# The two products of the channel-mixing block by seven block products instead of eight, in chunks of 768 tokens

## The chip, the cores and the metric

One core of a Trainium2 chip. The core has a matrix engine (TensorE; PE in the rows, its weight loads PEld), VectorE (DVE), ScalarE (ACT), GpSimd (POOL) and SyncE (SP), which in this kernel issues every DMA. The metric is the device time of one execution in microseconds, median of the runs.

## The reference, cut to what matters

Pooled attention, a first mixing block, then a second one; the change is in the last two lines of the second:

```python
def _moe2_ref(x, w_tok1, w_tok2, w_ch1, w_ch2):      # x: 8 x 576 x 512
    xt = x.transpose(0, 2, 1)
    h = np.maximum(xt @ w_tok1, 0.0) @ w_tok2
    u = x + h.transpose(0, 2, 1)
    h2 = np.maximum(u @ w_ch1, 0.0) @ w_ch2          # 512 x 1536, 1536 x 512
    return (u + h2).astype(np.float32)
```

The weights of both blocks come as 64-bit floats and are turned into 32-bit ones on the chip. There are 8 x 576 = 4608 tokens.

## The kernel before

Each big product is made of three matmuls on split operands: a number is held as a high part in the reduced type fp32r and a remainder, and high x high, high x low and low x high are added up in PSUM (HL3, line 61). All matmuls go through the helper mm, so all of them have line 159, transposes line 165; groups are told apart by the names of their tiles.

Stages: attention and first token mixing, batch by batch (lines 747 to 780); then for each of the 8 batches the first block's channel product (emit_ch, line 856), transposes (emit_tr), and the second block's token products (emit_tok1, emit_tok2), called from the loop at lines 1200 to 1218, where the next batch's u is loaded (load_u) and split (split_u, lines 853 and 854); the result goes to the DRAM buffer scr_x (line 918). In this text this second stretch, from about 553 to 776.6 us, is the token stage and one pass of its loop a batch.

The last stage (lines 1225 to 1235) takes the 4608 tokens in 9 chunks of 512. load_c fetches a chunk, split_c (lines 975 and 976) splits it, emit_c1 makes each of 12 hidden blocks of 128 rows from 12 matmuls and evicts it with a relu on ScalarE and a remainder on VectorE (lines 1003 and 1004), and emit_c2 makes each of 4 output blocks from 36 matmuls, adds u (line 1018) and stores (line 1019). The hidden result stays in SBUF. The weights are read as 64-bit words and converted in pieces of 256 or 288 columns by cq_step (VectorE lines 240 to 259, remainder on GpSimd or VectorE at line 287), partly in the token stage, partly in the first chunk.

SBUF tiles are named by tags, one buffer each, in one pool; a tile that takes over a tag waits for the last use of the one before. The eight PSUM banks are taken in turn by bank_any. Engines run in order; the order on each engine is set by a scheduler when the program is built, which starts from the order of the source but moves an instruction ahead when what it needs is there.

## Time and profile before

| | us |
|---|---|
| median of 3 runs | 1383.62 |
| lowest, highest | 1381.26, 1386.32 |
| span of the profiled execution | 1378.8 |
| of it the last stage, first to last matmul | 598.1 |

The profiled execution is known by its span; its own device time was not listed apart from the three runs. In the rows below, "x432" is a number of instructions, a tile name is the program's without its buffer number (so "m", "t", "x" stand for PSUM banks), and after "|" stand busy time, mean ns of one, and idle time before with what ended it. Windows list, after the length, the busy us of PE, PEld, DVE, ACT and POOL with the number of instructions, then the granted TensorE clock as a share of 2.4 GHz, the mean busy share of the 16 DMA engines, and GB/s.

### The profile page before, as it was taken

Reading aid. Unit: us, or ns where it says so; the run is one execution under the profiler, and the core shown is the slowest. Engines: PE = TensorE matmul, PEld = TensorE weight load, DVE = VectorE, ACT = ScalarE, POOL = GpSimd, SP = SyncE. Lnnn points to the kernel's source line nnn. Section 1 sums busy time; section 2 is a strip of 40 time slices with the busy share of each in tenths; the row PEclk is TensorE's granted clock in tenths of the full one; section 3 lists DMA queues with packets and bytes.
Section 4 is the critical chain, followed back from the end, with each engine's and each line's share of the span. In section 5 each row is a group of like instructions: output and inputs, shape, how many; then the busy total and the mean of one; then the engine's idle time right before and its main releaser. Section 6 shows DMA issues by size and latency. Waiting matters only on the chain.

```text
span 1378.8 us, 19219 instructions
## 1 busy us (share of the span) xinstructions
PE 1337.9 (97%) x7744; PEld 1179.0 (86%) x7744; DVE 708.7 (51%) x1473; ACT 441.5 (32%) x848; POOL 227.2 (16%) x251
## 2 busy tenths in 40 slices
PE   5999999999999999999999999999999999999998
PEld 3579999999999989899999888888888888888887
DVE  7698667595776898897445931212112221212120
ACT  4675455555545553242212321111111110102020
POOL 4363423243252442110000100000000000000000
PEclk9699999999999999999999999999999999999999
DMA  8324222132311124443211601010101010101000
GB/s 320 138 63 133 65 90 97 58 104 72 100 65 49 52 87 149 152 153 134 104 69 44 203 11 54 16 46 16 46 16 47 23 40 23 39 23 39 23 8 31
DMA packets 52297, 103.39 MB, mean 75 GB/s; under 512 B 5296, under 2 KB 6320, under 8 KB 52208
## 3 DMA queue, kind: packets, MB, share of 16 engines
q1 hardware_dynamic: 52208, 102.16, 22.1%
q8 instruction: 61, 1.00, 0.3%
q14 instruction: 28, 0.23, 0.1%
HBM read 73.83 MB, written 28.31 MB: 74 GB/s over the span
## 4 chain that ended last, share of the span: by engine, by line
PE 75%; DVE 16%; ACT 3%; issue 2%; DMA 2%; POOL 1%; SPq 0%; DVEq 0%; POOLq 0%; ACTq 0%
PE x L159 31%; PE m L159 21%; PE t L159 20%; PE x L165 2%; DVE sm L556 2%; DVE e L545 1%; DVE mx L544 1%; DVE tmp L725 1%; DVE sm L557 1%; DVE R L778 1%; DVE pt L595 1%; DMA stg<-w_ch 1%; DVE bdk L395 1%; DVE sums L402 0%; DMA bdk<-w_ch 0%
## 5 line engine op out<-in xcount | busy, mean ns | idle before, releaser
L159 PE MATMUL m<-wtk,Z 128*128 128x256 f32 (+1 forms) x1536 | 249.1, 301 | 9.4 <-DVE R L778 9.2
L159 PEld LDWEIGHTS m<-wtk,Z 128*128 128x128 f32 x1536 | 219.3, 191 | 12.2 <-DVE R L778 9.8
L159 PE MATMUL x<-Xh,wc 128*128 128x512 f32 x432 | 108.5, 392 | 0.0
L1003 ACT ACTIVATE gz<-m 128x512 fp32r<-128x512 f32 x18 | 10.7, 597 | 291.2 <-PE m L159 290.9
L159 PEld LDWEIGHTS x<-Xh,wc 128*128 128x128 f32 x432 | 81.0, 188 | 19.0
L740 POOL TENSOR_TENSOR Z<-tmp,Z 128x1024 fp32r<-128x1024 f32 x31 | 74.7, 2410 | 105.5 <-ACT Z L739 105.5
L159 PE MATMUL x<-gz,wc 128*128 128x512 f32 x324 | 91.5, 390 | 0.0
L1018 DVE TENSOR_TENSOR c<-x,c 128x512 f32<-128x512 f32 x18 | 12.4, 691 | 136.8 <-PE x L159 136.8
L159 PE MATMUL t<-wth,Xh 128*128 128x256 f32 (+1 forms) x504 | 76.3, 293 | 0.5 <-DVE Xh L528 0.2
L159 PEld LDWEIGHTS x<-gz,wc 128*128 128x128 f32 x324 | 60.8, 188 | 14.1
L159 PEld LDWEIGHTS t<-wth,Xh 128*128 128x128 f32 x504 | 66.9, 188 | 4.5 <-DVE Xh L528 1.8
L159 PE MATMUL x<-bdk,q 128*128 128x144 f32 x320 | 47.9, 303 | 14.9 <-DVE bdk L1055 7.0
L1004 DVE SCALAR_TENSOR_TENSOR gz<-x,gz 128x512 fp32r<-128x512 f32 x36 | 24.9, 691 | 67.0 <-ACT gz L1003 66.9
L159 PEld LDWEIGHTS x<-bdk,q 128*128 128x128 f32 x320 | 44.5, 203 | 17.2 <-issue 14.0
L159 PE MATMUL x<-Xl,wc 128*128 128x512 f32 x216 | 59.1, 395 | 0.0
L159 PE MATMUL m<-wtk,zt 128*128 128x256 f32 (+1 forms) x192 | 57.3, 298 | 0.0
L725 DVE TENSOR_TENSOR tmp<-x,tmp 128x1024 f32<-128x1024 f32 x32 | 39.0, 1219 | 31.3 <-ACT tmp L701 16.2
L159 PE MATMUL t<-Xh,wc 128*128 128x512 f32 x216 | 54.3, 393 | 0.0
L159 PE MATMUL m<-Xh,wc 128*128 128x512 f32 x216 | 54.2, 393 | 0.0
L707 DVE SCALAR_TENSOR_TENSOR tmp<-tmp,t 128x512 f32<-128x512 f32 x40 | 27.3, 682 | 47.4 <-ACT tmp L694 47.4
L561 POOL TENSOR_TENSOR e<-e,sm 128x720 f32<-128x720 f32 x32 | 45.2, 1413 | 27.8 <-DVE sm L560 26.1
L159 PEld LDWEIGHTS t<-Xh,wc 128*128 128x128 f32 x216 | 40.5, 188 | 9.5
(357 smaller groups left out, 2933.4 us busy)
## 6 DMA issues: line engine op xcount, KB each, us to landing
stg<-w_ch SPq DMA_DIRECT2D x38, 256.0 KB, 2.9
scr_u<-R SPq DMA_DIRECT2D x32, 288.0 KB, 2.1
u<-scr_u SPq DMA_DIRECT2D x32, 288.0 KB, 3.7
scr_x<-u SPq DMA_DIRECT2D x32, 288.0 KB, 2.3
c<-scr_x SPq DMA_DIRECT2D x36, 256.0 KB, 3.7
out<-c SPq DMA_DIRECT2D x36, 256.0 KB, 2.0
q<-qT SPq DMA_DIRECT2D x14, 640.0 KB, 3.9
kr<-kT SPq DMA_DIRECT2D x12, 576.0 KB, 3.9
```

The source lines that it names most:

```text
L159: nc.tensor.matmul(out=o, lhsT=l, rhs=r, start=start, stop=stop)
L165: nc.tensor.transpose(o, i, ident)
L395: nc.vector.tensor_copy(out=bdk[pr, 2 * g:2 * g + 2, 72 * e:72 * e + 72], in_=ks[pr])
L544: nc.vector.tensor_reduce(out=mx[:, c0:c1, :], in_=v, axis=AX.X, op=ALU.max)
L545: nc.vector.tensor_tensor(out=e[:, c0:c1, 2 * p:2 * p + 2, :], in0=v, in1=mx[:, c0:c1, :].unsqueeze(3).to_broadcast([128, n, 2, 72]), op=A ...
L556: nc.vector.tensor_reduce(out=sm, in_=ep, axis=AX.X, op=ALU.add)
L557: nc.vector.tensor_scalar(out=sm, in0=sm, scalar1=1e-9, scalar2=8.0, op0=ALU.add, op1=ALU.mult)
L561: nc.gpsimd.tensor_tensor(out=ep, in0=ep, in1=sm.unsqueeze(3).to_broadcast([128, 5, 2, 72]), op=ALU.mult)
L707: nc.vector.scalar_tensor_tensor(out=t, in0=t, scalar=MAGIC, in1=pt, op0=ALU.subtract, op1=ALU.subtract)
L725: nc.vector.tensor_tensor(out=tmp, in0=px.unsqueeze(1).to_broadcast([128, 2, 512]), in1=tmp, op=ALU.mult)
L740: later(1.0 if lo is nc.vector else 0.0, lambda: lo.tensor_sub(out=zl, in0=zv, in1=zh.bitcast(F32)), tg, zg)
L1004: nc.vector.scalar_tensor_tensor(out=g[:, 1, 0:n], in0=o, scalar=0.0, in1=g[:, 0, 0:n].bitcast(F32), op0=ALU.max, op1=ALU.subtract,)
```

## The change

Both products of the last stage are cut into 2 x 2 blocks: tokens in two halves of 384, contraction and output rows in halves. Seven products of sums and differences of blocks replace the eight block products; their results are combined when PSUM is evicted. A11, A12, A22 are blocks of the weights, S1 to S4 sums of such blocks; for each of them stands a like combination of the moving operand, made by moving().

Weights: weight_steps reads the 64-bit words of four blocks, converts them, forms the four sums, splits all seven into high and low part and stores them to DRAM (scr_w). These 72 steps are called one at a time by wstep between the groups of the token stage. The old conversions of these weights are gone.

channel_mix runs in a new pool that is laid over the old one, with waits per tile. It holds 34 buffers of 128 x 768 for moving operands, 12 of 128 x 384 for evictions and 21 weight tiles. First all six chunks go through the first product (first_pair: six groups of hidden rows, seven block products of six matmuls each); the hidden result goes to DRAM (scr_g). Then all six go through the second product (second_chunk), whose operands are read back from scr_g, combined and split again. pump takes the next steps of operand preparation from a queue whenever buffers are free. The weights of the second product replace those of the first in its last chunk.

```diff
-    sb = ctx.enter_context(tc.tile_pool(name="sb", bufs=1))
+    sbx = ExitStack()
...
+    NH = 384
+    NCH = NTOK // (2 * NH)
+    A12, A22, S1, S2, S3, S4, A11 = range(7)
+    PO = (A11, S2, A12, S1, S3, S4, A22)
+    scr_w = [dr.tile([128, 3, 7, 2, 2, 256], F32, name=f"scr_w{i}") for i in range(2)]
+    scr_g = [dr.tile([128, 4, 6, NH], F32, name=f"scr_g{c}") for c in range(NCH)]
...
+        def conv(i, kk):
+            if kk == 0:
+                raw[i][1] = wt_tile([128, 2, 2, 256], F32, f"wm{i}")
+            t = raw[i][0][kk]
+            m = raw[i][1][:, kk]
+            mu = m.bitcast(U32)
+            nc.scalar.activation(out=m, in_=t[:, :, :, 1].bitcast(F32), func=ACTF.Abs)
+            nc.vector.tensor_scalar(out=m, in0=m, scalar1=F64_FLOOR, scalar2=None, op0=ALU.max)
+            nc.vector.tensor_scalar(
+                out=mu, in0=mu, scalar1=3, scalar2=0x3FFFFFFF,
+                op0=ALU.logical_shift_left, op1=ALU.bitwise_and,
+            )
+            nc.vector.scalar_tensor_tensor(
+                out=mu, in0=t[:, :, :, 1], scalar=0xC0000000, in1=mu,
+                op0=ALU.bitwise_and, op1=ALU.bitwise_or,
+            )
+            nc.vector.scalar_tensor_tensor(
+                out=mu, in0=t[:, :, :, 0], scalar=29, in1=mu,
+                op0=ALU.logical_shift_right, op1=ALU.bitwise_or,
+            )
+        def sums(i):
+            m = raw[i][1]
+            s = raw[i][2] = wt_tile([128, 4, 256], F32, f"wsum{i}")
+            a11, a21, a12, a22 = m[:, 0, 0], m[:, 0, 1], m[:, 1, 0], m[:, 1, 1]
+            nc.gpsimd.tensor_tensor(out=s[:, 0], in0=a21, in1=a22, op=ALU.add)
+            nc.gpsimd.tensor_tensor(out=s[:, 2], in0=a11, in1=a21, op=ALU.subtract)
+            nc.vector.tensor_sub(out=s[:, 1], in0=s[:, 0], in1=a11)
+            nc.vector.tensor_sub(out=s[:, 3], in0=a12, in1=s[:, 1])
+        def split(i, half):
+            m, s = raw[i][1:3]
+            parts = ((m[:, 1], 2, nc.gpsimd), (m[:, 0, 0:1], 1, nc.gpsimd)) if half == 0 else (
+                (s[:, 0:2], 2, nc.vector), (s[:, 2:4], 2, nc.vector))
+            if half == 0:
+                raw[i][3] = {}
+            _, g, j = quads[i]
+            dst = scr_w[quads[i][0]]
+            for n, (src, k, eng) in enumerate(parts):
+                o = wt_tile([128, 2, 2, 256], F32R, f"wo{i}_{half}{n}")[:, 0:k]
+                nc.scalar.copy(out=o[:, :, 0], in_=src)
+                eng.tensor_sub(out=o[:, :, 1], in0=src, in1=o[:, :, 0].bitcast(F32))
+                o0 = (A12, A11)[n] if half == 0 else (S1, S3)[n]
+                nc.sync.dma_start(out=dst[:, g, o0:o0 + k, j], in_=o.bitcast(F32))
+        steps = [lambda: load(0)]
+        for i in range(len(quads)):
+            if i + 1 < len(quads):
+                steps.append(lambda i=i: load(i + 1))
+            steps += [lambda i=i: conv(i, 0), lambda i=i: conv(i, 1), lambda i=i: sums(i),
+                      lambda i=i: split(i, 0), lambda i=i: split(i, 1)]
+        return steps
...
+    def channel_mix(sc):
+        layout = ["b%d" % i for i in range(3)] + ["ev%d" % i for i in range(12)] + [
+            "b%d" % i for i in range(20, 30)] + ["wa%d" % i for i in range(7)] + [
+            "b%d" % i for i in range(3, 14)] + ["b%d" % i for i in range(30, 34)] + [
+            "b%d" % i for i in range(14, 18)] + ["wa7", "wa8", "b18", "b19"] + [
+            "wa%d" % i for i in range(9, 21)]
+        shapes = {"b": [128, 2, NH], "e": [128, NH], "w": [128, 2, 2, 256]}
+        for tag in layout:
+            sc.tile(shapes[tag[0]], F32, tag=tag, name=tag)
+        free_b = ["b%d" % i for i in range(34)]
+        free_e = ["ev%d" % i for i in range(12)]
+        free_w = ["wa%d" % i for i in range(21)]
+        class Buf:
+            def __init__(self, pool, dt, name):
+                self.pool = pool
+                self.tag = pool.pop(0)
+                self.t = sc.tile(shapes[self.tag[0]], dt, tag=self.tag, name=name)
...
+        def load_w(m, o, g):
+            w = weights[m, o, g] = Buf(free_w, F32R, f"wa{m}_{o}_{g}")
+            nc.sync.dma_start(out=w.t.bitcast(F32), in_=scr_w[m][:, g, o])
...
+        def split(key, x):
+            h, l = buf("h", F32R), buf("l", F32R)
+            ops[key] = (h, l)
+            nc.scalar.copy(out=h.t, in_=x.t)
+            nc.vector.tensor_sub(out=l.t, in0=x.t, in1=h.t.bitcast(F32))
+        def sub(o, x, y):
+            nc.vector.tensor_sub(out=o.t, in0=x.t, in1=y.t)
...
+            groups = [
+                [sp(A11, "11", False)],
+                [(0, t1), (1, t2), sp(S2, "t2", False)],
+                [sp(A12, "21", False), (0, t4)],
+                [sp(S1, "11", True)],
+                [(0, t3), sp(S3, "12", True)],
+                [sp(S4, "22", True)],
+                [sp(A22, "21", True)],
+            ]
+            return [ld(b) for b in ("11", "12", "22", "21")], groups
+        queue = []
+        def pump(n):
+            while queue and n > 0 and queue[0][0] <= len(free_b):
+                queue.pop(0)[1]()
+                n -= 1
...
+        for c in range(NCH):
+            loads, groups = moving(load_x(c), (0, c))
+            queue += loads + [s for g in groups for s in g]
...
+        def product(o, xs, first, last, cont):
+            seq = [(wx[wi], x[a]) for a, wi in HL3 for wx, x in xs]
+            for i, (l, r) in enumerate(seq):
+                mm(o, l, r, first and i == 0, last and i == len(seq) - 1, cont)
+        pump(15)
+        for g in range(3):
+            for o in PO:
+                load_w(0, o, g)
+        order2 = [(o, g) for o in PO for g in range(3)]
+        pump(4)
...
+        def first_pair(c, i):
+            g = i // 2
+            cs = slice((i % 2) * 128, (i % 2) * 128 + 128)
+            fin = c == NCH - 1
+            def prod(o, ps, first):
+                w = weights[0, o, g].t
+                h, l = ops[0, c, o]
+                xs = [((w[:, k, 0, cs], w[:, k, 1, cs]), (h.t[:, k], l.t[:, k])) for k in range(2)]
+                product(ps, xs, first, True, not first)
+                if i == 5:
+                    h.free()
+                    l.free()
+                if fin and i % 2 == 1:
+                    weights[0, o, g].free()
+                    load_w(1, *order2.pop(0))
+                pump(1 if not fin else 2)
+            def put(k, e):
+                nc.sync.dma_start(out=scr_g[c][:, k, i], in_=e.t)
+                e.free()
+            X = bank_any()[:, 0:NH]
+            prod(A11, X, True)
+            p1 = evac("p1")
+            nc.scalar.copy(out=p1.t, in_=X)
+            Y = bank_any()[:, 0:NH]
+            prod(S2, Y, True)
+            u2 = evac("u2")
+            nc.vector.tensor_add(out=u2.t, in0=Y, in1=p1.t)
+            p1.free()
+            prod(A12, X, False)
+            e = evac("g11")
+            nc.scalar.activation(out=e.t, in_=X, func=ACTF.Relu)
+            put(0, e)
+            W = bank_any()[:, 0:NH]
+            prod(S1, W, True)
+            p5 = evac("p5")
+            nc.scalar.copy(out=p5.t, in_=W)
+            Z = bank_any()[:, 0:NH]
+            prod(S3, Z, True)
+            nc.vector.tensor_add(out=p5.t, in0=Z, in1=p5.t)
+            nc.gpsimd.tensor_tensor(out=p5.t, in0=p5.t, in1=u2.t, op=ALU.add)
+            nc.scalar.activation(out=p5.t, in_=p5.t, func=ACTF.Relu)
+            put(3, p5)
+            prod(S4, W, False)
+            e = evac("g12")
+            nc.vector.tensor_add(out=e.t, in0=W, in1=u2.t)
+            nc.scalar.activation(out=e.t, in_=e.t, func=ACTF.Relu)
+            put(1, e)
+            prod(A22, Z, False)
+            e = evac("g21")
+            nc.vector.tensor_add(out=e.t, in0=Z, in1=u2.t)
+            u2.free()
+            nc.scalar.activation(out=e.t, in_=e.t, func=ACTF.Relu)
+            put(2, e)
...
+        def load_o(c, d, k, t):
+            e = evac("o")
+            t0 = (2 * c + t) * NH
...
+        def second_chunk(c):
+            D = range(2)
+            def prod(o, ps, first):
+                for ph in range(3):
+                    w = weights[1, o, ph].t
+                    h, l = ops[1, c, ph, o]
+                    for d in D:
+                        cs = slice(d * 128, d * 128 + 128)
+                        xs = [((w[:, k, 0, cs], w[:, k, 1, cs]), (h.t[:, k], l.t[:, k])) for k in range(2)]
+                        product(ps[d], xs, first and ph == 0, ph == 2, not first)
+                    h.free()
+                    l.free()
+                    pump(3)
...
+            X = banks()
+            u11 = [load_o(c, d, 0, 0) for d in D]
+            prod(A11, X, True)
+            p1 = [evac("p1") for _ in D]
+            for d in D:
+                nc.scalar.copy(out=p1[d].t, in_=X[d])
+            Y = banks()
+            prod(S2, Y, True)
+            u2 = [evac("u2") for _ in D]
+            for d in D:
+                nc.vector.tensor_add(out=u2[d].t, in0=Y[d], in1=p1[d].t)
+                p1[d].free()
+            prod(A12, X, False)
+            u22 = [load_o(c, d, 1, 1) for d in D]
+            for d in D:
+                nc.vector.tensor_add(out=u11[d].t, in0=X[d], in1=u11[d].t)
+                store_o(c, d, 0, 0, u11[d])
+                nc.gpsimd.tensor_tensor(out=u22[d].t, in0=u22[d].t, in1=u2[d].t, op=ALU.add)
...
+            prod(S4, W, False)
+            for d in D:
+                nc.vector.tensor_add(out=u12[d].t, in0=W[d], in1=u12[d].t)
+                store_o(c, d, 0, 1, u12[d])
+            prod(A22, Z, False)
+            for d in D:
+                nc.vector.tensor_add(out=u21[d].t, in0=Z[d], in1=u21[d].t)
+                store_o(c, d, 1, 0, u21[d])
+        for c in range(NCH):
+            second_chunk(c)
...
@@ -1168,14 +1448,8 @@
             interleave(mix_steps(b), side)
         flush()
         cq_step(20)
-        n = [int(x + 0.5) for x in P["a_n"]]
-        cq_use(("stg0", "stg1", "bdk"), ("cvt0", "vlr"))
-        lo_m[0] = max(2, n[0])
-        cq_mode[0] = min(2, int(P["md"][1] + 0.5))
-
-        add_wc1()
-        add_wc2(range(4))
-        cq_load()
+        wq[:] = weight_steps()
+        wstep(2)
         def ch(b):
             order = [(j, th) for j in range(4) for th in range(2)]
@@ -1186,8 +1460,7 @@
                 if b == 0 and P["a_tr"] == i:
                     emit_tr(0, 0)
                     emit_tr(0, 1)
-                if i in P["a_cq"]:
-                    cq_step()
+                wstep()
         if B > 1:
             load_u(1)
@@ -1207,32 +1480,17 @@
             for j in range(4):
                 for th in range(2):
                     emit_tok2(b, j, th)
+                    if th == 0:
+                        wstep()
                     if j == 1 and th == 0 and b + 1 < B:
                         for c in range(5):
                             emit_tr(b + 1, c)
                 if b + 2 < B:
                     split_u(b + 2, j)
-            if b == B - 1:
-                load_c(0)
-                for j in range(4):
-                    split_c(0, j)
-
-        cq_step(100)
-        add_wc2(range(4, 12))
-        cq_load()
-        if len(chunks) > 1:
-            load_c(1)
-        for c in range(len(chunks)):
-            for f in range(12):
-                emit_c1(c, f)
-                cq_step(2)
-            cq_step(100)
-            for j in range(4):
-                emit_c2(c, j)
-                if c + 1 < len(chunks):
-                    split_c(c + 1, j)
-            if c + 2 < len(chunks):
-                load_c(c + 2)
+        wstep(1000)
+        flush()
+        sbx.close()
+        channel_mix(ctx.enter_context(tc.tile_pool(name="sc", bufs=1, reuse_waits="tile")))
 def _layout(inputs):
```

## Rows read from the trace of the kernel before

**Rows 1.** The page's first part: each engine's busy us, share of the span, instructions.

```profile
PE 1337.9 (97%) x7744; PEld 1179.0 (86%) x7744; DVE 708.7 (51%) x1473; ACT 441.5 (32%) x848; POOL 227.2 (16%) x251
```

**Rows 2.** The chain of waits in order of time, last stage: start us, length us, what.

```profile
776.83 2.79 PE m L159 x12
...
1358.38 16.59 PE x L159 x72
1374.99 0.69 DVE c L1018
```

**Rows 3.** Windows, last stage: length, busy us per engine (count), granted clock, DMA share, GB/s.

```profile
776.60:1375.00 598.40, 598.36 (x2594) 486.39 (x2592) 134.22 (x226) 84.52 (x149) 4.83 (x6) 1.00 0.10 34
```

**Rows 4.** Timeline of TensorE in the token stage: start us, us, instruction.

```profile
643.20 0.28 PE L159 MATMUL t<-wk2a,h1a 128*128 128x256 f32 x1
...
643.90 0.30 PE L159 MATMUL x<-wk2a,h1a 128*128 128x320 f32 x1
...
644.77 0.28 PE L159 MATMUL x<-wk2a,h1a 128*128 128x256 f32 x1
```

**Rows 5.** Groups by line, weight loads: busy us, mean ns of one, idle before.

```profile
L159 PEld LDWEIGHTS x<-Xh,wc 128*128 128x128 f32 x432 | 81.0, 188 | 19.0
```

**Rows 6.** Groups by line and shape, VectorE.

```profile
L976 DVE TENSOR_TENSOR Xl<-c,Xh 128x512 fp32r<-128x512 f32 x36 | 23.3, 685 | 12.0 <-PE x L159 12.0
...
L778 DVE TENSOR_TENSOR R<-m,R 128x320 f32<-128x320 f32 x32 | 15.5, 483 | 13.0 <-PE m L159 13.0
...
L244 DVE TENSOR_SCALAR vlr<-vlr 128x256 f32<-128x256 f32 x27 | 8.2, 305 | 0.3
```

**Rows 7.** Timeline, two VectorE operations one behind the other.

```profile
757.69 0.68 DVE L882 TENSOR_TENSOR x<-m,x 128x512 fp32r<-128x512 f32 x1
...
758.29 0.68 DVE L882 TENSOR_TENSOR x<-t,x 128x512 fp32r<-128x512 f32 x1
```

**Rows 8.** Windows, token stage: a batch with weight conversions and one without.

```profile
600.00:627.60 27.60, 27.60 (x193) 26.37 (x192) 26.85 (x73) 9.43 (x20) 3.70 (x5) 1.00 0.47 159
682.00:710.00 28.00, 28.00 (x195) 26.69 (x194) 14.10 (x28) 6.14 (x11) 0.00 (x0) 1.00 0.25 91
```

**Rows 9.** Timeline, VectorE beside GpSimd: two pairs that overlap.

```profile
504.02 2.39 POOL L740 TENSOR_TENSOR Z<-tmp,Z 128x1024 fp32r<-128x1024 f32 x1 [1.16 <-ACT Z L739]
504.16 2.46 DVE L259 SCALAR_TENSOR_TENSOR late<-bdk,late 128x192 uint32<-128x192 uint32 x1
...
605.09 0.74 POOL L287 TENSOR_TENSOR wc<-cvt,wc 128x256 fp32r<-128x256 f32 x1 [3.56 <-ACT wc L285]
605.14 0.68 DVE L901 SCALAR_TENSOR_TENSOR h1b<-t,h1b 128x512 fp32r<-128x512 f32 x1
```

**Rows 10.** Groups by line and shape, GpSimd.

```profile
L740 POOL TENSOR_TENSOR zt<-tmp,zt 128x512 fp32r<-128x512 f32 x8 | 10.3, 1292 | 49.5 <-ACT zt L739 49.5
```

**Rows 11.** Timeline of SP's queue at the end of the token stage.

```profile
767.29 1.75 SPq L968 DMA_DIRECT2D c<-scr_x  x4
...
773.17 4.59 SPq L918 DMA_DIRECT2D scr_x<-u  x4
```

**Rows 12.** DMA issues by line: count, KB each, median us to landing.

```profile
c<-scr_x SPq DMA_DIRECT2D x36, 256.0 KB, 3.7
```

**Rows 13.** Windows around a gap in TensorE's work.

```profile
508.00:512.00 4.00, 2.31 (x17) 1.87 (x16) 4.00 (x9) 1.77 (x3) 1.29 (x1) 0.99 0.28 82
512.00:516.00 4.00, 3.37 (x17) 3.08 (x16) 3.93 (x11) 0.73 (x2) 2.30 (x3) 0.58 0.26 74
```

**Rows 14.** Timeline: a group's relu begins after the next group's first matmul.

```profile
1003.82 2.00 PE L159 MATMUL x<-Xh,wc 128*128 128x512 f32 x8
1004.02 0.60 ACT L1003 ACTIVATE g<-t 128x512 fp32r<-128x512 f32 x1 [2.18 <-PE t L159]
```

**Rows 15.** Groups by line and shape, ScalarE.

```profile
L975 ACT CAST Xh<-c 128x512 fp32r<-128x512 f32 x36 | 20.6, 616 | 10.3 <-PE x L159 9.9 <-DMA c<-scr_x 0.3
```

**Rows 16.** Windows, busiest DMA stretch of the prologue.

```profile
20.00:28.00 8.00, 5.91 (x20) 2.66 (x18) 7.70 (x18) 5.25 (x13) 3.65 (x7) 1.00 1.04 409
```

205 lines of the change are left out of this document (114 added, 91 removed).

## The prediction

> **What bounds the kernel now.** The first view to read is the page's busy line: TensorE is busy for 97% of the span, VectorE for half of it [rows 1]. A share is an average, so the last stage is read by itself. In the chain of waits every piece from 776.83 us to 1374.97 us is TensorE, and only the last VectorE addition and its store follow [rows 2]. The window over this stage gives 598.36 us of TensorE in 598.40 us, at full clock (2.4 GHz), with DMA engines 10% busy and VectorE 134 us [rows 3]. So TensorE's matmul stream is the bound, and whatever else the stage does is hidden. It holds 9 chunks x (12 x 12 + 4 x 36) = 2592 matmuls of 512 columns, which makes 598.2 / 2592 = 0.2308 us each.
>
> **Part 1, the matmuls.** After: 6 chunks of 768 tokens, each cut into 2 x 2 blocks of 384 tokens. The first product is 6 column groups x 7 block products x 6 matmuls, the second 7 x 3 x 2 x 6, so 252 + 252 per chunk and 3024 in all, of 384 columns: 7/8 of the columns in 7/6 of the matmuls. The trace has no 384. In a token group six matmuls of 256 columns take 643.90 - 643.20 = 0.70 us and the next six of 320 take 0.87 us [rows 4], 0.1167 and 0.145 us each. Between 320 and 512 the slope is (0.2308 - 0.145)/192 = 0.447 ns a column, so 384 costs 0.145 + 64 x 0.447 ns = 0.1736, and I take 0.174. Ends: 0.173 (in proportion to 512) and 0.175 (in proportion to 256). A weight load is recorded at 188 ns [rows 5], longer than this, but 256-column matmuls run every 117 ns with the same loads, so loads overlap and don't set the pace. Sum: 3024 x 0.174 = **526.2 us** (523 to 529), 72 us less.
>
> TensorE: Matmul & The Clock Gate in the Trainium skill (Back-to-back issue gap) gives N/2.4 + 2.5 ns for a warm isolated matmul; worked out from it, an estimate, 384 columns take 162.5 ns and the total would be 35 us lower. Its 215.8 ns for 512 columns is contradicted by the row's 230.8, so the measurement decides.
>
> **Part 2, weight sums in the token stage.** The old conversions of these weights, partly in the token stage and partly in the first chunk, go; they were hidden, so that gains nothing. Twelve steps per batch (two of 12 blocks of weights) take their place over some five batches. VectorE per block: four tensor_scalar and four scalar_tensor_tensor of 512, two subtractions of 256, two of 512. A 512 subtraction is recorded at 0.685, 320 columns at 0.483, a 256 tensor_scalar at 0.305 [rows 6], but two 512s in a row start 0.60 apart [rows 7], so about 0.085 of each overlaps. Block: 4 x 0.35 + 4 x 0.60 + 2 x 0.335 + 2 x 0.60 = 5.7 us; two per batch 11.3. A batch without conversions costs VectorE 14.1 of 28.0 us; one with conversions is at 26.9 of 27.6, and TensorE lost nothing in it [rows 8]. So 25.4 of 27.6 fits, barely. GpSimd gets two sums of 256 and subtractions of 512 and 256 per block, 3 x 0.74 [rows 9] + 1.29 [rows 10] = 3.5 us, 7.0 a batch, and it can hold VectorE up: a 192-column VectorE operation took 2.46 us, because it began 0.14 us into a 2.39 us GpSimd operation; one that reads PSUM kept its 0.68 us beside a GpSimd operation [rows 9]. If 60% of 7.0 us falls so (the part of VectorE's 25.4 that doesn't read PSUM, by my count), VectorE has 29.6 us for 27.6 and each of five batches is some 2 us late, minus slack: **+8** (0 to 25: every GpSimd us lost). Each block issues 2 loads and 4 stores on SP; the stores wait for splits, with the loads of the next batch's u queued behind, a batch ahead of need, so nothing.
>
> SBUF — State Buffer in the Trainium skill (Who interferes with whom) has the shared port pair as an exclusive lock, for operations with two SBUF inputs too; the trace agrees, with those 2.46 us. By that rule the upper end would hold.
>
> **Part 3, the start.** The new tiles lie over the old ones. SP does not keep the program's order: the old stage's first loads were issued at 767.29, ahead of the last token stores at 773.17 [rows 11]. So most of the 21 weight tiles (512 KB each) can come early. By my count of tile sizes wa0, the very first weight, overlaps the end of kr, which the last token matmuls read. Its load starts then: about 4 us, from 3.7 us for 256 KB [rows 12], and the clock may fall to 1.2 GHz as after the gap at 508 us (granted 0.58 in the next 4 us [rows 13]), 2 us. **+6** (0 to 25; the upper end is rival B).
>
> **Part 4, the first product.** TensorE refills a bank one block product (6 x 0.174 = 1.04 us) after it left it; between lies an eviction that starts 0.2 us after the group and takes under 0.6 [rows 14]. It collides only with a 768-column operand copy (0.616 x 1.5 = 0.92 us at most by [rows 15]), at most 0.4 us, about 5 times a chunk: **+4** (0 to 12). VectorE: 11 x 0.87 (768 columns: 0.685 + 256 x 1.05 ns - 0.085) + 24 x 0.47 = 21 of 44 us. SP's stores wait for ScalarE's relu, with the next chunk's operand loads behind; these run a chunk ahead. In the last chunk 21 new weights, stores and reloads make 20 MB, 50 us at the 409 GB/s of [rows 16] against 44; the last are needed 25 us later: **+3** (0 to 12).
>
> **Part 5, the second product.** Operands come back from DRAM and are formed three times as often: 33 operations of 768 and 10 evictions, 33 x 0.87 + 10 x 0.47 = 33.4 of 44 us of VectorE, plus up to 8 GpSimd additions of 1.0 us in its way, 41. The 34 buffers hold at worst 15 raw blocks and three products' operands, a lead of two products (12.6 us) over a landing of 4 us. **+6** (0 to 30: 5 us a chunk with no lead). Removed splits and evictions were hidden: nothing. The end, one addition and one store, stays.
>
> **Sum.** 1378.8 - 598.1 = 780.7; + 526.2 + 8 + 6 + 4 + 3 + 6 = 1333.9 of span. The median of the runs shown is 4.8 us above the profiled span, which I add: **1339 us**. The measurement tells apart about 0.3%, 4 us.
>
> **Rivals.** A, everything hides better: parts 2 to 5 cost 0 to 5 together: 1312 to 1317.
> B, all tiles wait for the end of the old pool. Then 21 weights and two chunks of x, 14.2 MB, take 35 us at 409 GB/s, 42 at the 338 GB/s that 159 GB/s at 0.47 busy imply [rows 8]; the third group's eviction buffers wait for the first stores, queued behind, with 20 us of TensorE work done by then. Loss 18 to 25 instead of 6: 1351 to 1358. Against it: loads slip ahead of stores now [rows 11].
> C, the lead in part 5 is lost: +24, 1363. It decides once fewer than six buffers are free when a product starts; my count says 13.
> D, slower: DRAM traffic. A second chunk moves 4.7 + 1.6 + 1.6 MB in 44 us, 180 GB/s, in lines of 1536 bytes, which no busy stretch of the trace shows. If bytes count, 409 GB/s stand ready; if lines count, 338 x 1536/2304 = 225. It turns slower under 152 GB/s (52 us a chunk); at 120 it is 66 us a chunk and 1471.
> E, GpSimd takes all of its 7.0 us a batch from VectorE: 5 x 4.8 = 24 us for 8: 1355. The hold-up is in the trace, but most of VectorE's other 14.1 us a batch read PSUM, which the second pair of [rows 9] shows unharmed. In the Trainium skill it is the rule of SBUF — State Buffer named above, in full.
> F, the change doesn't shrink the matmul time: each takes its weight load's 188 ns: 3024 x 0.188 = 568.5, 1381, no change. Against it: 256 columns every 117 ns [rows 4].
>
> **Chances.** Forecast (1320 to 1352) 50%, A 3, B 15, C 12, E 10, D 7, F 3. The range takes in B, C and E and leaves out D, F and most of A: 1317 to 1371. Faster 0.87 (the forecast, A, B, C, E less 3 for several together), same 0.05 (F and part of those), slower 0.08 (D and the rest).
>
> **What would show it.** Six matmuls of a new product in 1.04 us (F: 1.13). VectorE below 95% in the batches after 553 us and no TensorE idle there over 10 us in all (E). The first weight loads on SP before the last token stores (B: after, with 20 us of idle TensorE). Second chunks of 44 to 46 us, waits there on VectorE (C) or on DMA landings (D). The prediction is wrong if TensorE has over 45 us of idle time after 553 us.

## The result and the profile after

The changed kernel takes 1342.85 us, median of four runs (1337.88 to 1347.63), against 1382.44 for the kernel before on the same chip; the recorded ratio of the two is 0.9725, 95% interval 0.9673 to 0.9777. The prediction was 1339, range 1317 to 1371, faster with 0.87. It holds, 3.9 us off. That hides larger errors that stand against each other: two terms of the sum were too small, two too large.

The executions of most kernels here, the kernel before among them, fall into two groups some 10 us apart, two and two of them for after, so that its median lies between 1338.30 and 1347.39, where none of them lies. So the 3.9 us are in part luck, and where a few us matter, the profiled executions are compared stage by stage and not by their medians. The profiled execution of after is the slowest of its four (1347.63, span 1345.9).

The page's first part, each engine's busy us, share and count (before: [rows 1]):

```profile
PE 1279.4 (95%) x8176; PEld 1222.5 (91%) x8176; DVE 963.7 (72%) x1649; ACT 621.1 (46%) x1136; POOL 356.1 (26%) x351
```

The chain of waits has TensorE in pieces of 36 matmuls, and windows over most of the last stage (length, busy us per engine and count, granted clock, DMA share, GB/s; before: [rows 3]) have it without a gap:

```profile
1103.83 6.24 PE x L160 x36
1116.31 6.24 PE x L160 x36
```

```profile
1036.00:1080.00 44.00, 43.82 (x253) 43.50 (x252) 23.17 (x35) 20.36 (x42) 7.25 (x6) 1.00 0.89 323
1094.00:1182.00 88.00, 88.00 (x508) 87.73 (x507) 75.97 (x85) 35.31 (x49) 22.59 (x16) 1.00 0.59 194
1182.00:1270.00 88.00, 87.97 (x505) 86.95 (x504) 75.80 (x87) 36.12 (x51) 21.17 (x16) 1.00 0.55 178
1270.00:1342.40 72.40, 72.28 (x416) 71.75 (x415) 49.27 (x57) 22.37 (x31) 20.66 (x16) 1.00 0.36 119
```

A matmul of 384 columns costs 6.24 / 36 = 0.1733 us; the last three windows give 248.25 / 1429 = 0.1737. VectorE is at 86% in the first two of them, 76 of 88 us, and the DMA engines at 55 to 59%; neither holds TensorE up. So the matmuls are where the gain comes from, as forecast, and most of what was lost was lost ahead of 860 us, in two places.

The first is the token stage. Its first matmul is the same in both kernels (before first, then after):

```profile
551.48 1.10 PE L159 MATMUL m<-Xh,wch 128*128 128x256 f32 x8
547.35 1.11 PE L160 MATMUL m<-Xh,wch 128*128 128x256 f32 x8
```

From there to the end of the last token matmul before takes 776.83 - 551.48 = 225.35 us and after 789.97 - 547.35 = 242.62, which is 17.3 us more. Windows over the stage, in the same columns (before: [rows 8], where TensorE is busy throughout):

```profile
553.00:580.00 27.00, 24.38 (x159) 22.06 (x158) 26.91 (x49) 13.04 (x24) 8.01 (x9) 1.00 0.80 278
606.00:634.00 28.00, 25.34 (x162) 23.43 (x162) 27.23 (x50) 12.66 (x22) 7.47 (x8) 0.94 0.85 301
662.00:690.00 28.00, 23.91 (x158) 22.81 (x157) 27.09 (x48) 13.66 (x26) 10.14 (x10) 0.91 0.75 270
```

VectorE is busy for 97 to 100%, TensorE for 85 to 91%. The waits of TensorE from 540 to 780 us are all for VectorE, nearly all for its evictions, 13.4 us with the two smaller groups (the kernel before has 2.4 us of waits there):

```profile
PE t L166 <- DVE u L868: 4.8, 3, 2.1
PE x L166 <- DVE u L868: 4.5, 5, 2.3
PE m L166 <- DVE u L868: 2.4, 2, 1.9
```

The timeline shows what fills VectorE, a sum of 256 elements that reads two SBUF tiles and starts 0.07 us into a GpSimd operation:

```profile
616.57 1.26 POOL L1000 TENSOR_TENSOR wo<-wm,wo 128x512 fp32r<-128x512 f32 x1
616.64 1.48 DVE L986 TENSOR_TENSOR wsum<-wsum,wm 128x256 f32<-128x256 f32 x1 [0.45 <-POOL wsum L984]
```

It ends at 618.12, 0.29 us after GpSimd's. The eleven of 553 to 690 us take 1259 ns in the mean; the shortest of all twelve took 422.

The granted clock of 0.94 and 0.91 in the second and third window is a loss of its own. It falls behind waits that stand close together, as here (TensorE's two waits, then windows of 4 us over them and behind them):

```profile
682.93 0.33 PE L166 MATMUL x<-con,u 128*128 128x128 f32 x1 [2.28 <-DVE u L868]
685.84 0.47 PE L166 MATMUL t<-con,u 128*128 128x128 f32 x1 [1.81 <-DVE u L868]
```

```profile
682.00:686.00 4.00, 1.26 (x9) 1.02 (x10) 3.46 (x6) 3.38 (x7) 2.00 (x2) 0.84 1.01 345
686.00:690.00 4.00, 4.00 (x18) 4.00 (x19) 4.00 (x9) 4.00 (x9) 0.00 (x0) 0.50 0.66 249
```

TensorE's busy time at the lower level from 618 to 624 and from 684 to 692 us makes some 4 us lost, an estimate from windows of 2 us (busy time times what is missing in the clock). The kernel before has a granted clock of 1.00 throughout this stage.

The second place is the start of the last stage. TensorE's timeline has the last token matmul and the first of the product, and the second stall 27 us on; SP's queue shows what was issued when (before: [rows 11], where the next stage's loads went ahead of the last token stores):

```profile
789.66 0.31 PE L160 MATMUL x<-wk2b,h1b 128*128 128x320 f32 x1
799.61 1.62 PE L160 MATMUL m<-h,wa 128*128 128x384 f32 x4 [9.64 <-ACT h L1059]
...
826.95 0.83 ACT L1059 CAST h<-r 128x768 fp32r<-128x768 f32 x1 [3.60 <-DMA r<-scr_x]
833.00 0.48 ACT L1196 ACTIVATE g<-m 128x384 f32<-128x384 f32 x1
833.53 0.69 PE L160 MATMUL m<-h,wa 128*128 128x384 f32 x1 [6.59 <-ACT g L1196]
```

```profile
786.30 4.54 SPq L919 DMA_DIRECT2D scr_x<-u  x4
790.94 1.97 SPq L1121 DMA_DIRECT2D r<-scr_x  x4
793.00 22.93 SPq L1051 DMA_DIRECT2D wa<-scr_w  x21
816.90 4.19 SPq L1121 DMA_DIRECT2D r<-scr_x  x4
```

No load of the stage is issued before the last token store. Then four blocks of x, 21 weight tiles and the next chunk's blocks stand in one queue. TensorE idles for 9.64 us. The row names ScalarE's rounding for this, but the operands of the first product were ready by 796.6, and in other runs with the same start (e3, e4, e9) the same wait is put to the first weight (here e3's):

```profile
PE m L160 <- DMA wa<-scr_w: 9.6, 1, 9.6
```

At 826.95 ScalarE rounds a block of the second chunk, which came behind the 21 weights, ahead of the eviction (L1196, 833.00) that TensorE needs, and TensorE idles for another 6.59. After each gap the granted clock is at the lower level for a while (windows after the first):

```profile
800.00:802.00 2.00, 2.00 (x8) 2.00 (x8) 2.00 (x4) 1.05 (x3) 0.00 (x0) 0.50 1.03 414
802.00:804.00 2.00, 2.00 (x8) 2.00 (x7) 2.00 (x4) 0.58 (x2) 0.00 (x0) 0.50 1.03 406
804.00:806.00 2.00, 2.00 (x13) 2.00 (x12) 1.98 (x3) 1.13 (x2) 0.00 (x0) 0.96 1.01 401
```

144 matmuls take 27.3 us from 799.6 to 826.9 where 144 x 0.1733 = 25.0, and 138 take 26.5 from 833.5 to 860 where 23.9: 4.9 us for the clock. Together the start lost 9.6 + 6.6 + 4.9 = 21.1 us.

### The profile page after: what moved, and what is told of

Read it like the earlier page. It is cut to its first block, busy times and chain, and to the rows that moved or that the text cites. A ratio compares the mean times of both kernels' runs of the same rounds, so it can differ in the third digit from the quotient of the medians.

```text
span 1345.9 us, 21938 instructions
## 1 busy us (share of the span) xinstructions
PE 1279.4 (95%) x8176; PEld 1222.5 (91%) x8176; DVE 963.7 (72%) x1649; ACT 621.1 (46%) x1136; POOL 356.1 (26%) x351
## 5 line engine op out<-in xcount | busy, mean ns | idle before, releaser
L160 PE MATMUL x<-h,wa 128*128 128x384 f32 x1008 | 218.1, 337 | 0.5 <-DVE p L1204 0.4
L160 PEld LDWEIGHTS x<-h,wa 128*128 128x128 f32 x1008 | 178.4, 189 | 4.1 <-DVE p L1204 2.1
L1060 DVE TENSOR_TENSOR l<-r,h 128x768 fp32r<-128x768 f32 x144 | 150.5, 1062 | 37.8 <-ACT h L1059 35.2
L1059 ACT CAST h<-r 128x768 fp32r<-128x768 f32 x144 | 115.7, 835 | 97.6 <-DVE l L1060 58.9
L160 PE MATMUL m<-h,wa 128*128 128x384 f32 x576 | 125.9, 339 | 18.5 <-ACT h L1059 9.6
L160 PE MATMUL x<-l,wa 128*128 128x384 f32 x504 | 128.5, 336 | 0.0
L160 PEld LDWEIGHTS m<-h,wa 128*128 128x128 f32 x576 | 102.9, 190 | 20.7 <-ACT h L1059 9.9
L160 PE MATMUL t<-h,wa 128*128 128x384 f32 x432 | 93.1, 336 | 0.0
L160 PEld LDWEIGHTS x<-l,wa 128*128 128x128 f32 x504 | 91.3, 188 | 0.0
L160 PEld LDWEIGHTS t<-h,wa 128*128 128x128 f32 x432 | 77.0, 189 | 0.0
```

Source lines behind the costliest of these rows:

```text
L160: nc.tensor.matmul(out=o, lhsT=l, rhs=r, start=start, stop=stop, skip_group_check=skip)
L1059: nc.scalar.copy(out=h.t, in_=x.t)
L1060: nc.vector.tensor_sub(out=l.t, in0=x.t, in1=h.t.bitcast(F32))
```

## The experiments

Theory: the two losses are (1) VectorE filled to the brim by the weight preparation with GpSimd's hold-up on top, and (2) transfers that do not start before the last token store. Below, "token" is the time from the token stage's first matmul to the end of its last, "ends" is when that last one ends, and "stage" the time from there to the end of the last matmul, all in the profiled execution; "before" is the kernel before on the same chip. "ends" depends also on when the token stage began, which differs by 4.1 us between e10 and e11 (548.67 and 552.79), whose programs are alike up to there; so "token" is the one to compare.

| run | median us | before | ratio, 95% interval | token | ends | stage |
|---|---|---|---|---|---|---|
| kernel before | 1383.62 | | | 225.4 | 776.8 | 598.1 |
| after | 1342.85 | 1382.44 | 0.9673 to 0.9777 | 242.6 | 790.0 | 552.3 |
| after_again | 1348.68 | 1381.35 | 0.9721 to 0.9808 | 241.3 | 789.6 | 553.5 |
| e1_spread | 1349.88 | 1382.45 | 0.9736 to 0.9786 | 242.3 | 790.3 | 553.0 |
| e2_late_w | 1347.04 | 1382.45 | 0.9731 to 0.9761 | 241.6 | 790.7 | 549.3 |
| e3_pool_dve | 1332.80 | 1382.45 | 0.9599 to 0.9650 | 227.6 | 776.0 | 552.3 |
| e4_noprep | 1332.06 | 1382.45 | 0.9621 to 0.9650 | 222.5 | 772.4 | 554.9 |
| e9_paced | 1340.90 | 1380.94 | 0.9648 to 0.9744 | 231.4 | 783.0 | 555.0 |
| e6_early | 1337.83 | 1381.35 | 0.9674 to 0.9735 | 241.3 | 792.2 | 539.6 |
| e7_early_dve | 1325.63 | 1381.35 | 0.9565 to 0.9639 | 225.3 | 772.8 | 547.0 |
| e8_early_late_dve | 1327.74 | 1381.35 | 0.9572 to 0.9657 | 225.4 | 776.9 | 546.3 |
| e10_best | 1319.45 | 1380.94 | 0.9533 to 0.9604 | 224.7 | 773.3 | 539.3 |
| e11_pump | 1313.93 | 1382.61 | 0.9456 to 0.9514 | 225.6 | 778.4 | 534.0 |
| e5_buf28 | 1357.72 | 1380.94 | 0.9773 to 0.9884 | 243.0 | 793.2 | 562.1 |

After was timed again beside three of them:

> The changed kernel itself, on the same chip as the three runs beside it, so that they can be compared with it directly: 1338 to 1348 us, ratio to the kernel before 0.970 to 0.976.

Its trace agrees with the first within 1.4 us in each column; median and ratio are just above what was expected, and the interval of the ratio reaches to 0.9808. 1348.68 is the footing for the others. e1 to e4 ran on another chip than after_again; there e1, which turned out to be the same program, took 1349.88.

**e1_spread: the preparation thinned out in the source.**

```diff
-                    if th == 0:
+                    if th == 0 and j == 0:
                         wstep()
```

> The steps of the weight preparation go nine to a batch (eight beside the channel products, one beside the token products) in place of twelve, so the same work reaches from the second batch to the last instead of ending in the sixth. Theory S, saturation: the token stage lost 13.3 us (its last matmul ended at 789.97 us, 776.6 in the kernel before) because VectorE was full, 97 to 99% of each stretch from 553 to 690 us; with a quarter of the load moved to the batches that have room VectorE falls to about 90% there, the last token matmul comes at 777 to 781 us, and the kernel takes 1330 to 1335 us where the changed one takes 1342.85. Rival T, per step: each block of weights costs about 1.1 us wherever it stands (13.3 us over 12 blocks: its instructions go ahead of the token stage's evictions in VectorE's order); the last token matmul stays at 788 to 791 us and the time within 3 us of the changed kernel's.

Nothing moved, as T has it. But the trace shows that the edit did nothing: TensorE, VectorE, ScalarE and GpSimd have their instructions in the same order as in after, and the twelfth block's sums come behind 40 evictions of the channel product (line 868, eight a batch), 5.0 batches, in both. The scheduler moves an instruction up as soon as its inputs are there, and the preparation's are. So this run decides nothing between S and T, and a place in the source is no control over when such work runs.

**e3_pool_dve: GpSimd's part on VectorE.** The sums and remainders `nc.gpsimd.tensor_tensor` and `tensor_sub` of lines 984, 985 and 1000 become `nc.vector`, four operations a block:

```diff
-            nc.gpsimd.tensor_tensor(out=s[:, 0], in0=a21, in1=a22, op=ALU.add)
-            nc.gpsimd.tensor_tensor(out=s[:, 2], in0=a11, in1=a21, op=ALU.subtract)
+            nc.vector.tensor_tensor(out=s[:, 0], in0=a21, in1=a22, op=ALU.add)
+            nc.vector.tensor_tensor(out=s[:, 2], in0=a11, in1=a21, op=ALU.subtract)
```

> The four GpSimd instructions of each block of weights (two sums, two remainders, 3.5 us of GpSimd for a block) run on VectorE, where they add about 1.6 us for a block by the rate of VectorE's own sums. Theory L, lock: VectorE's instructions beside them are stretched (a sum of 256 elements takes 1259 ns where 0.42 us are its own), about 1.8 us for a block; moving the four takes as much away as it adds, VectorE's busy time stays within 5 us of 963.7, its 256-element sum falls to 0.4 to 0.5 us, and the time stays within 4 us of the changed kernel's. Rival N: the stretch is small or would lie in VectorE's idle time; then 12 x 1.6 = 19 us are added to a full engine, and the kernel takes 1355 to 1362.

1332.8 us, 16 less than after_again and 17 less than e1: N is wrong, and L right in its parts and wrong in its total. VectorE's group of line 986 (line, operation, count, busy us, mean ns), first in after, then here:

```profile
L986 DVE TENSOR_TENSOR wsum<-wsum,wm 128x256 f32<-128x256 f32 x11 | 13.9, 1259 | 2.2 <-POOL wsum L984 2.2
```

```profile
L986 DVE TENSOR_TENSOR wsum<-wsum,wm 128x256 f32<-128x256 f32 x10 | 4.2, 417 | 0.0
```

VectorE does 48 operations more, 12 x (0.415 + 0.418 + 0.685 + 0.417) = 23.2 us by their rows, and its busy time falls from 963.7 to 960.2. So GpSimd had cost it 23.2 + 3.5 = 26.7 us, 2.2 for a block. The evictions of line 868, which read PSUM, take 414 ns for 256 columns in after and 418 here: not touched. SBUF — State Buffer in the Trainium skill (Who interferes with whom) has it so: a VectorE operation with two inputs in SBUF contends with a GpSimd one that reads SBUF, and one with at most one, outside VectorE's two-port modes, does not. Both halves agree with these rows. The operation of line 966, with one input in SBUF, is slowed all the same, from 418 ns for 512 columns here to 572 in the mean in after; whether by the exception for those modes no run shows.

Why then did the time fall, with VectorE no less busy in all? Windows of this run:

```profile
606.00:634.00 28.00, 28.00 (x196) 26.74 (x196) 27.38 (x60) 12.07 (x23) 0.00 (x0) 1.00 0.81 289
634.00:662.00 28.00, 28.00 (x196) 26.72 (x195) 27.92 (x62) 12.91 (x24) 0.00 (x0) 1.00 0.82 284
```

VectorE is as full as in after, and TensorE loses nothing. By the same count as in e1 the twelve blocks reach over 6.0 batches, in after over 5.0. The scheduler packed as many blocks into a batch as the instructions' own lengths allow; in after GpSimd's hold-up came on top. That this is how it reckons is inferred; the next run tests what follows from it.

**e9_paced: GpSimd kept, the blocks held apart.** A copy of one element makes each block wait for the token group last evicted in the source, and two of eight places for a step are left out in the channel products:

```diff
             m = raw[i][1][:, kk]
+            nc.gpsimd.tensor_copy(out=m[:, 0, 0:1], in_=last_u[0])
...
-                wstep()
+                if i % 4 != 2 or b == 0:
+                    wstep()
```

> The changed kernel with the preparation held back: GpSimd copies one element of the token group last evicted into each block's tile before the conversion writes it, so that no block can start before its place in the source. By the order of VectorE's instructions the twelve blocks now reach over 7.0 batches of token work; in the changed kernel, and in the run that only moved the steps in the source, they reach over 5.0, and in the run with GpSimd's four operations on VectorE over 6.0. GpSimd keeps its four operations for a block, with all they take from VectorE. Theory S, saturation: VectorE was over its time in each batch (2.25 blocks in 28 us at 6.4 us each, beside 14.2 of other work, make 28.6) and TensorE paid the difference; at 1.75 blocks a batch VectorE is at 14.2 + 1.75 x 6.4 = 25.4 of 28 us, about 90%, the idle time of TensorE between 553 and 780 us falls from 14 to 0 to 4 us, and the kernel is 9 to 13 us faster than the changed kernel on the same footing (1348.7): 1336 to 1340. Rival T: each block costs TensorE 1.1 us by way of GpSimd, wherever it stands (an eviction beside a GpSimd operation is late, and a bank with it); the idle time stays at 10 to 14 us, and the time at 1345 to 1350.

TensorE's waits from 540 to 780 us fall from 13.4 to 5.2, the granted clock stays at 1.00 in the token stage, which is 9.8 us shorter than in after_again; the time is 7.8 us lower, just above S's range. In its windows VectorE is at 25.95 and 22.75 of 28, with the 256-element sum still at 1233 ns:

```profile
606.00:634.00 28.00, 26.73 (x182) 25.05 (x181) 25.95 (x51) 12.15 (x22) 9.11 (x12) 1.00 0.74 268
634.00:662.00 28.00, 27.47 (x191) 26.07 (x191) 22.75 (x46) 10.81 (x20) 4.93 (x8) 1.00 0.78 265
```

So of the 15.9 us that the token stage of after_again is longer than that of the kernel before, 9.8 go when the same operations are spread out: they came of too much work in too few batches. The spreading takes part of the hold-up away too, since VectorE's busy time over the token stage is 192.1 us here and 197.0 in after_again; fullness and hold-up are not parted by this run. 6.1 us are left, 5.2 of them waits (2.4 in the kernel before), and whether these come from fullness within a few us or from single late evictions stays open.

**e4_noprep: the price of the whole preparation.** The float64 weights are loaded and all pieces stored, but from one rounded tile; conversion, sums and remainders are left out.

```diff
-                o = wt_tile([128, 2, 2, 256], F32R, f"wo{i}_{half}{n}")[:, 0:k]
-                nc.scalar.copy(out=o[:, :, 0], in_=src)
-                eng.tensor_sub(out=o[:, :, 1], in0=src, in1=o[:, :, 0].bitcast(F32))
-                nc.sync.dma_start(out=dst[:, g, o0:o0 + k, j], in_=o.bitcast(F32))
+                nc.sync.dma_start(out=dst[:, g, o0:o0 + k, j], in_=wo[0][:, 0:k].bitcast(F32))
```

> The weight preparation's arithmetic is left out: the float64 weights are loaded and the same 84 pieces stored as before, but all from one rounded tile, so the last stage multiplies by wrong weights; ScalarE, VectorE and GpSimd have none of the conversion, sums and remainders. It shows the whole price of that arithmetic in the token stage. Theory S: the 13.3 us of the token stage are this arithmetic on a full VectorE; the last token matmul comes at 770 to 777 us and the kernel is 13 to 19 us faster, 1324 to 1330 (more than 13.3, since the kernel before converts its weights too, in one part of them later). Rival M: the token stage is longer because of the stores and loads of the preparation (DMA), and loses 8 us or more of its 13 still: the time is 1335 or above.

The last token matmul ends at 772.4 and TensorE waits for nothing from 540 to 780 us: S, and not M. The absolute time is 2 us above S's range, which was reckoned from 1342.85; from after_again it is 16.6 less. It is no faster than e3: the token stage ends 3.6 us earlier, the last stage is 2.6 longer.

**e2_late_w: the second stall, by order of the loads.**

```diff
-        for g in range(3):
-            for o in PO:
-                load_w(0, o, g)
+        for o in PO:
+            load_w(0, o, 0)
         order2 = [(o, g) for o in PO for g in range(3)]
-        pump(4)
...
+                if c == 0 and i in (0, 2):
+                    load_w(0, o, i // 2 + 1)
```

> Only the seven weight tiles of the first group are loaded ahead of the first chunk's products; the other fourteen follow in that chunk's first pairs, behind the loads of the second chunk's blocks in SyncE's order. Theory Q, queue order: the second stall at the start of the stage (6.59 us at 826.9 to 833.5, with the clock at 0.50 to 0.71 until 840) came from ScalarE, which stood in order at the rounding of a block of the second chunk, and that block's load lay behind 21 weight tiles on SyncE; with seven ahead it arrives some 14 us earlier (14 tiles x 0.25 MB at 400 GB/s is 9 us by an estimate from the stretch 793 to 816), the second stall and its slow clock vanish, and the kernel is 7 to 9 us faster, 1334 to 1336. The first gap (9.64 us at 789.97 to 799.61) stays at 9 to 10 us. Rival R: the second stall is the DMA engines' capacity and not the order; the fourteen tiles then stall the products a little later by the same 4 to 7 us, and the time stays within 3 us.

The single stall breaks up into six waits of at most 1.2 us for ScalarE: they make 4.0 us between the first product and 860 us, where it was 6.6, and the clock stays up behind them. The stage is 3 to 4 us shorter; the time is 1.6 us under after_again's and 2.8 under e1's, within R's 3 us. (A weight tile is 512 KB and not the 0.25 MB of the expectation, so 14 of them are 18 us at 400 GB/s.) The DMA engines are at 1.02 to 1.04 from 800 to 840, so the same bytes come late in another order. R is nearer in the size, though TensorE waits here for ScalarE too and not for weights; e11 goes on from here.

**e6_early: eight tiles ahead of the boundary.** Eight tags of the token stage lie in a pool of their own that outlives it; before the last batch they take four blocks of x and four weight tiles. This leaves 33 buffers of 768 columns for 34.

```diff
-        return sb.tile(shape, dt, tag=tag, name=name or tag)
+        return (pw if tag in [f"w{i}" for i in range(8)] else sb).tile(shape, dt, tag=tag, name=name or tag)
...
+            if b == B - 1:
+                wstep(1000)
+                load_early()
```

> Eight of the token stage's tiles are kept in a pool of their own that lives on into the last stage; as soon as the weight preparation is done they take the four raw blocks of the first chunk and the first four weight tiles, loaded ahead of the last batch. Theory B, the boundary: the 9.64 us in which TensorE stands before the first product are the transfers that can start only after the last token store (SyncE's first load of the stage came at 790.94, after the store at 786.30); with these eight there before, the gap falls to 0 to 2 us, the clock does not fall in 794 to 804, and the kernel is 10 to 14 us faster than the changed kernel, 1329 to 1333. The second stall (6.6 us) is still there, or shorter by the 3.5 MB that no longer stand in the queue. Rival W: the first product waits in truth for the last token group's result or for the rounding of its operands on ScalarE and VectorE, whose inputs come with the last batch; then the gap stays above 6 us and the gain is under 5 us. A second rival: the remaining 17 weight tiles still fill the DMA engines for 22 us, and the second stall grows by what the first one loses; gain 3 to 6 us.

```profile
791.91 0.31 PE L161 MATMUL x<-wk2b,h1b 128*128 128x320 f32 x1
792.06 0.86 PE L161 MATMUL m<-h,wr 128*128 128x384 f32 x4
```

The gap is gone (lines are numbered one higher here, from 1030 on by 24 at most), the granted clock is 1.00 from 790 to 820, the stage is 13 to 14 us shorter and the median 10.9 lower than after_again's (the token stage began 2.6 us later). B it is, though its absolute range, reckoned from 1342.85, was missed. Since the early tiles have a pool of their own and a place of their own in the source, the run does not tell which of the two held the loads back before. The second stall stays, 6.9 us.

**e7_early_dve and e8_early_late_dve: both cures**, with eleven early tiles, which leaves 32 buffers; e8 has e2's order too.

> Both: the GpSimd instructions of the preparation on VectorE, and eleven early tiles (four raw blocks, all seven weight tiles of the first group). In the run with VectorE alone the token stage ran without the losses of the changed kernel, and 9.6 + 7.3 us of idle TensorE were left at the start of the last stage. If the two are independent the gains add: 1332.8 less 10 to 16 us is 1317 to 1323. If they are not (the early loads want tiles of the preparation, which now ends later, 718 for 703 us, but well ahead of the last batch at about 740): 1324 to 1330.

> As the run before it, and the weights of the second and third group are loaded in the first chunk's first pairs, behind the loads of the second chunk. If order on SyncE's queue is what makes the second stall, this one has none and takes 4 to 8 us less than the run before it, 1311 to 1317. If the DMA engines' capacity is what makes it (the late weights alone moved the stall and gained about 2 us in the profile), with eleven tiles out of the way there is capacity enough in either order, and the two agree within 3 us.

e7 takes 1325.63: the gain is some 4 us less than the two added up (1348.68 less 15.9 and 10.9 is 1321.9). TensorE's waits behind 860 us show where the rest went, a wait for the sums of the second product that after hardly has (0.4 us for VectorE in all):

```profile
PE x L161 <- DVE p L1307: 6.4, 4, 2.4
```

The second stall is 2.9 us in e7. e8 agrees with e7 within 2.1 us: with these tiles out of the way the order of the other weights makes no difference that can be told.

**e10_best: nine early tiles and 33 buffers, as many as e6**, with e3's edit. On e6:

```diff
-        for n, o in enumerate(PO[0:4]):
+        for n, o in enumerate(PO[0:5]):
```

> GpSimd's four operations on VectorE and nine early tiles (four raw blocks, five weight tiles), which leaves 33 buffers in place of the 32 of the run with eleven. If the 6.4 us of waits in the second product there were for want of buffers, they fall to 0 to 2 us, while the second stall at the start grows by the two weight tiles that load late (1 MB at 410 GB/s, 2.5 us, an estimate from the stretch 780 to 790 of that run): 2 to 4 us faster than it, 1321 to 1324. If buffers are not the cause, the time is that of the run with eleven or 2 to 3 us above, 1325 to 1329.

```profile
PE m L161 <- ACT g L1220: 5.8, 1, 5.8
```

```profile
PE x L161 <- DVE p L1307: 0.4, 1, 0.4
```

The wait for the sums of the second product is 0.4 us, the second stall 5.8; 1319.45 us, below both ranges. The 6 us against e7 agree with one buffer more than 32: in e7 VectorE stood 1.69 us for a block read back and then formed the next operands ahead of the sum that TensorE waited for. But the two runs differ in the early weight tiles too (seven and five), and e5 below, with 28 buffers, hasn't this wait at all; so that the buffer was the cause is not shown.

**e11_pump: the second chunk's loads and rounding later.** On e10:

```diff
-        pump(4)
...
-                pump(1 if not fin else 2)
+                if c > 0 or i > 2:
+                    pump(1 if not fin else 2)
```

> The run with nine early tiles and GpSimd's operations on VectorE, in which the second chunk's blocks are loaded and rounded only from the fourth pair of products of the first chunk on, in place of from its start. It asks what the second stall is (5.8 us there, put down to ScalarE's eviction). Theory H, head of the queue: ScalarE evicts the products in order behind the rounding of a block of the second chunk, whose load stands behind the weights on SyncE; nothing that TensorE needs is late in itself. With the rounding behind the first three pairs' evictions the stall goes, the granted clock stays at 1.0 in 800 to 820, and the kernel takes 5 to 9 us less than 1319.45: 1310 to 1314. Rival K, capacity: the products wait in truth for weight tiles of the second and third group that are still on their way; then 4 to 6 us of the stall stay, whatever ScalarE does. A second rival: the operands of the second chunk, formed in half the time, come late, and 3 to 8 us are lost at that chunk's start, near 820 to 850.

The wait of 5.8 us is gone from the list, 2.6 us for ScalarE's copies stand in its place, the clock is 1.00 throughout 780 to 860, and the stage is 5.3 us shorter (its token stage ended 5 us later than e10's, 4.1 of it because it began later, so the two profiled executions take the same in all; the medians are 5.5 us apart). H: with five weight tiles there before, the others came in time, and TensorE had waited for an eviction behind a rounding that nobody needed yet. Of the second rival's 3 to 8 us near 820 to 850 there are 2.4 us of idle TensorE, between 820 and 840, and its waits are for ScalarE's copies and not for late operands. 1313.93 us is some 5% under the kernel before, and the last stage is within 10 us of 3024 x 0.1733 = 524.

**e5_buf28: rival C's buffers.**

```diff
-        free_b = ["b%d" % i for i in range(34)]
+        free_b = ["b%d" % i for i in range(28)]
```

> The operands of the last stage have 28 buffers of 768 columns in place of 34. It asks how far the feed of the second product is from deciding. By the count of the prediction 13 are free when a product starts and fewer than six decide: with 28 there are seven, and the time stays within 3 us of the changed kernel's 1348.7. Rival: the count is too good. With 32 buffers (the run with eleven early tiles) TensorE waited 6.4 us in the second product for the sums of its results, where the changed kernel waits 0 to 1.5; then 28 cost 15 to 40 us, in waits that fall between 1094 and 1342 us, and the time is 1364 to 1389.

9.0 us more than after_again in the median, 8.6 in the stage: over the 3 of the one, under the 15 of the other. The margin is thinner than counted, but it doesn't break off. The waits are for ScalarE's evictions and lie in both products, not in the second alone (lines 1188 and 1201 are of the first, 1277 of the second):

```profile
PE m L160 <- ACT p L1188: 4.3, 5, 1.0
PE m L160 <- ACT p L1277: 4.2, 3, 1.6
PE x L160 <- ACT p L1201: 2.9, 3, 1.0
```

## Why the prediction was right, step by step

- **Part 1, the matmuls: right.** 0.174 us forecast, 0.1733 to 0.1737 measured, so the interpolation of [rows 4] held; 36 in 6.24 us rule out F, for which 36 would be 6.77. 598.1 us of last stage became 552.3, of which 524 to 525 are matmuls.
- **Part 2, the weight sums: right in mechanism, +8 forecast, 17.3 measured** (the token stage takes 242.62 us for 225.35). 11.0 of it are waits of TensorE (13.4 for 2.4), some 4 the lower clock behind them, and some 2 were not placed. E's sign, VectorE above 95% and over 10 us of idle TensorE, was met, at some 70% of E's price. The hold-up was forecast at 60% of 3.5 = 2.1 us a block and is 2.2. Two steps were off. One is "two blocks per batch": five batches of two make ten blocks and not twelve, and the scheduler packed all twelve into 5.0 batches. The other is the clock, for which this part had no term. E's full rule, every GpSimd us, was too much: GpSimd's twelve blocks took 49.6 us in after, of which 26.7 reached VectorE. Spread over 7.0 batches, the same operations cost 6.1.
- **Part 3, the start: wrong, +6 forecast, 21.1 measured.** The failing step is "most of the 21 weight tiles can come early". In [rows 11] loads had slipped ahead of the last stores; here none did. Rival B, at 15%, had the right size (18 to 25) and the right first half: 9.6 us to the first weight, with no load ahead of the last token store. Whether the tiles of the old pool held the loads back, as B says, or their place in the queue, no run shows. The second half I had put to eviction buffers that wait for stores; the trace and e11 put it to ScalarE, in order behind a rounding whose block came behind the weights.
- **Part 4, the first product: +7 forecast, 2.7 measured**, all of it waits for ScalarE and VectorE in 860 to 1080 us. The exchange of the weights runs at 323 GB/s, 0.89 of the DMA engines, in the window of 1036 to 1080, and costs nothing.
- **Part 5, the second product: +6 forecast, 0 measured**: TensorE has 248.25 of 248.40 us (after_again has 1.5 us of waits there). C and D did not come. D's fear of short lines is gone with the 194 GB/s at a DMA share of 0.59 in the window from 1094 us. C's count of buffers was too good: 13 were to be free and six to decide, and six taken away (e5), which by that count should cost nothing, cost 9 us, in waits for ScalarE in both products and not in C's waits for VectorE in the second. What the count missed was not followed.
- **The sum.** The terms beside the matmuls were 8 + 6 + 7 + 6 = 27 and came to 17.3 + 21.1 + 2.7 + 0 = 41.1, which is 14.1 more. The span is 1345.9 for 1333.9, 12 us off: the token stage began 4.1 us earlier than in the kernel before (547.35 for 551.48), for which there was no term and which e10 and e11 show to be as large between programs that are alike, and some 2 us were not placed. So by the span the miss is 15.1 us in part 3, 9.3 in part 2, and 10.3 the other way in parts 4 and 5, 4.1 by that start. The time is off by less still because the 4.8 us added for what lies between span and median had the other sign here: the median of after lies 3.1 us below its profiled span. That the forecast came within 3.9 us is luck; that it came within its range is not, since the matmuls gave the 72 us that were forecast (598 less 524 to 525 is 73 to 74). TensorE's idle time behind 553 us is 13.4 + 16.2 + 2.7 = 32.3 us, under the 45 that were to make the prediction wrong.

## What to carry to other kernels

When a stage gives way to one with other tiles, ask of each first load where it stands on its queue and which buffer it can land in while the old stage still runs: a few persistent tiles for the first operands were worth more here than anything inside the new stage. Work put "beside" a stage stands where the scheduler puts it and not where the source has it (e1); see what GpSimd beside it does to its length, and hold it apart by a dependence (e9). And don't let an in-order engine prepare the next chunk ahead of an eviction of this one as long as the next chunk's data are still in the queue.

## What the runs showed of the hardware that was not expected

- VectorE's share is no measure of harm: at 27.92 of 28 us TensorE lost nothing (e3), at 27.23 it lost 2.7 (after).
- The DMA engines moved 368 GB/s at a share of 1.00 under a TensorE that was busy for 44.00 of 44 us, in the chunk of e11 in which all weights are exchanged:

```profile
1016.00:1060.00 44.00, 44.00 (x256) 44.00 (x255) 23.11 (x33) 23.21 (x42) 5.65 (x5) 1.00 1.00 368
```

- Gaps of 9.64 and 6.59 us went with the lower clock level (granted 0.50), and so did two waits of 2.28 and 1.81 us with TensorE busy for 1.26 of 4.00 us around them (after, 682 to 686); waits of 2.4 us in all between 820 and 840 us in e11 left it at 1.00.
- GpSimd seems to be held up too: its two sums of 256 elements, 0.73 and 0.74 us at their shortest, took 0.85 and 0.93 in the mean in after; no run takes VectorE away from beside them.
